# A segment-recurrent attention block with its gradients on one core: W_k held in two tiles, scaled O stored from GpSimd's queue, and the last forward step reordered

## Chip, core and metric

The kernel runs on one core of a Trainium2 chip. The metric is device time in microseconds (us) of one execution; lower is better. The engines are TensorE (PE in the profile; its weight loads are PEld), VectorE (DVE), ScalarE (ACT), GpSimd (POOL) and SyncE (SP), which issues most of the transfers. Transfers that GpSimd issues go through a queue of their own (q0, software), those of SyncE through another (q1, hardware).

## The reference

The program computes a transformer block and all its gradients. `x` is 2048 rows of 512; the attention part works in 64 segments of 32 rows, and 8 rows of memory go from one segment to the next, so the segments are a chain:

```python
mod = (_silu(c) @ w_mod).reshape(c.shape[0], 6, 1, -1)      # sa, ca, ga, sb, cb, gb
h = _layernorm(x, axis=-1) * (1 + ca) + sa
x = x + ga * _A_ref(h, A_mem0, A_Wq, A_Wk, A_Wv, A_Wo, A_seg_len)
h = _layernorm(x, axis=-1) * (1 + cb) + sb
x = x + gb * _B_ref(h, B_w_gate, B_w_up, B_w_down)
...
for s in range(n_seg):                                      # inside _A_ref, H = 32 heads of 128
    h = jnp.concatenate([mem, xs], axis=1)                  # 8 + 32 rows
    q = jnp.einsum('btd,dhe->bhte', h, Wq)
    k = jnp.einsum('btd,dhe->bhte', h, Wk)
    v = jnp.einsum('btd,dhe->bhte', h, Wv)
    p = _softmax(scores, axis=-1)                           # scores masked
    o = jnp.einsum('bhqk,bhke->bhqe', p, v)
    o = jnp.einsum('bhte,hed->btd', o, Wo)
    mem = o[:, :M, :].copy()
    outs.append(o[:, M:, :])
...
h = _sigmoid(g) * u                                         # _B_ref: g = x w_gate, u = x w_up
return jnp.einsum('bsf,fd->bsd', h, w_down)
```

The outputs are the block's result and the gradients of `x`, the memory, all weights and the modulation, for a given gradient of the result.

## The kernel before

One program in stages, on one core.

**Setup** (to about 50 us) loads the weights (W_q, W_k and W_v are 4 MB each) and starts the modulation vectors. `W_q` and `W_k` come in through a helper that loads heads 24 to 31 into a side tile first and later places them with VectorE copies (`place`).

**Forward loop** (`for s in range(NS)`, 64 steps of about 14 us, to about 950): q, k and v of one segment (`pass_ps` products with Wk, Wq and Wv in PE), scores `st_ps`, their exponentials `ET` (L902), the row sums and P V products `or_ps` (L906, L926), the scaled O `Ost` (VectorE L957 and ScalarE L954, by the reciprocal `rden`, L911), its transposes `tps` (L918), and the output product `at_ps` with Wo. `Ost` has one buffer. For the backward pass each step also stores scaled O as rows (`OSR`, L1089), O transposed (`OT`, L1127), V transposed (`VT`, L1154) and P (`PS`, L1155): 352 KB each, all in SyncE's queue, in which the two DMA transposes of the step stand too (VTr, L1051, and Pst, L1059). P is transposed by a DMA and scaled on GpSimd one step later (`norm`, L1152). The memory rows come back through `at_ft` and `hT`. In every fourth step a row tile of 128 rows goes through its first norm, and GpSimd stores it (`H1ROWS`, L419). Sixteen loads of modulation weights (`wmod_r`, L195) are spread over the loop.

**The last step, s = 63**, is written out apart: in it the weights of the second part are loaded over those of the first (`w_gate`, L996, and `w_up`, L1061, over Wk; `w_down`, L1086, over Wv), the first row tile of the second part is prepared (`first_tile`: its norm's power on GpSimd L776, its scaling on VectorE L779, a cast on GpSimd L780), step 62's P is scaled (L1152), and step 63's own P is transposed by PE (`turn_p`) and scaled by VectorE (`scale_p`, L946), then stored (L1160). The rows of the next tiles are loaded by `glu_load` (L1188 to L1191) in SyncE's queue.

**Second part** (950 to 1284): 16 row tiles forward and backward through w_gate, w_up and w_down; `hh` is transposed by a DMA (`hhT`, L1357, SyncE's queue) for the product with w_down (L1379). Then its weight gradients (L1583, to 1456), beside which the transposed weights of the backward loop are made by PE transposes (`wtp`, L1677).

**Backward loop** (1456 to about 2430): the segments in reverse. The first step's loads `Pst_l`, `VT_l`, `OT_l` (L1830), `Qst` and `Kst` (L1845) go into space that the second part has used; the pools p4ld (loads), p4pt and p4rx lie one behind the other, p4ld first, over Wv's space. `g_ps` (L1923) needs Pst_l and `dOst`, which GpSimd copies (L1968). A step's dq, dk and dv go out as rows (`DQR`, `DKR`, `DVR`, 352 KB each) in GpSimd's queue. At the end of a step the gradient of the memory rows is summed: the product `dhq_ps` with its last piece (`foldsel`), split in two halves `dh_hi` (ScalarE) and `dh_lo` (VectorE), folded by PE (`dh_ft`), copied to `dyT` (ScalarE, L2049), on which the next step's products wait. `proj_b` is a product of 16 matmuls (`pass_ps<-WoT,dyb`), which in most steps fills PE where it would wait.

**Last stage** (to 2974): the weight gradients of the attention.

The order of each engine's instructions is that in which the program issues them; `pin` keeps a scheduler from moving them. A transfer waits in its engine's order, so all that stands behind a waiting transfer of SyncE waits too.

Of the kernel before, what the change touches and what calls it, by code (L numbers as in the profile page):

```python
# [7 lines left out]
BF16 = mybir.dt.bfloat16  # L8
# [32 lines left out]
class K:  # L41
# [145 lines left out]
    def mod_rest(self, psp, pool, k):  # L187
# [5 lines left out]
        def load():  # L193
            st["w"] = pool.tile([128, DC, 128], BF16, name="wmod_r", bufs=1)
            nc.sync.dma_start(st["w"][:], self.io["w_mod"].rearrange("(cc p) n -> p cc n", p=128)[:, :, sl])  # L195
# [51 lines left out]
    def col_pass(self, psp, w, hf, lhs, rows, eng, ps=None, cs=None, steps=None):  # L247
# [5 lines left out]
        for c in cs or range(DC):  # L253
            wc = w[:, c, :].rearrange("p (h e) -> p h e", e=E)
# [14 lines left out]
    def load_heads(self, t, w, src, parts=1):  # L269
# [4 lines left out]
        n = 24 // parts  # L274
        for i in range(parts):
            nc.sync.dma_start(w[:, :, i * n * E:(i + 1) * n * E], src[:, :, i * n:(i + 1) * n, :].rearrange("p c h e -> p c (h e)"))

        def place():
            i = 24
            for hl in range(3):  # L280
                m = 3 if hl < 2 else 2
                nc.vector.tensor_copy(w[:, :, i * E:(i + m) * E].rearrange("p c (h e) -> p c h e", e=E),
                                      t[:, :, hl:hl + 3 * (m - 1) + 1:3, :])
                i += m
# [164 lines left out]
    def phase2(self):  # L449
# [9 lines left out]
        Wk = self.Wk = wvk.tile([128, DC, H * E], BF16, name="Wk")  # L459
# [5 lines left out]
        with ExitStack() as ctx:  # L465
# [391 lines left out]
            for s in range(NS):  # L857
# [178 lines left out]
                if s == NS - 1:  # L1036
                    v_chunk(s, 2)
                    first_tile[5]()
                st_exp(0)
# [20 lines left out]
                else:  # L1060
                    nc.gpsimd.dma_start(self.w_up, io["B_w_up"].rearrange("(c p) f -> p c f", p=128))  # L1061
# [23 lines left out]
                if s == NS - 1:  # L1085
                    nc.gpsimd.dma_start(self.w_down, io["B_w_down"].rearrange("(fc p) d -> p fc d", p=128))  # L1086
                    for g0, t, w in ((0, RAs[0]["k"], 8), (8, RAs[0]["q"], G - 8)):
                        nc.sync.dma_start(self.VT[s, :, g0:g0 + w, :], t[:, 0:w * GW].rearrange("p (g x) -> p g x", x=GW))
                nc.sync.dma_start(self.OSR[s], gl3(Ost))  # L1089
                at_ps = outproj()  # L1090
                if s == NS - 1:
                    nc.sync.dma_start(self.OT[s], gl3(OT))
# [4 lines left out]
                    parts = self.split_pair(sb2, at_ps, "at")  # L1097
                    while tail.pieces:
# [7 lines left out]
                    self.pop_later()  # L1106
                    self.pop_later()
                    turn_p(1)
                    self.pop_later()
                    for pi in (2, 0, 1):  # L1110
                        scale_p(pi)
# [35 lines left out]
                self.store_rows(psp, sb2, ft, self.AOA[s + 1, 0:32, :], "at", "p")  # L1147
                if s4 == nseg_t - 1:
# [11 lines left out]
            nc.sync.dma_start(self.PS[NS - 1], Pst[:])  # L1160
# [3 lines left out]
    def glu_tiles(self):  # L1164
# [6 lines left out]
        in_k = [self.flat(Wk, 2 * n + i * D, D) for i in range(4)]  # L1171
# [3 lines left out]
        self.w_gate = self.flat(Wk, 0, n).rearrange("p (c f) -> p c f", c=DC)  # L1175
        self.w_up = self.flat(Wk, n, n).rearrange("p (c f) -> p c f", c=DC)
# [17 lines left out]
    def phase3(self):  # L1194
# [9 lines left out]
        with ExitStack() as ctx:  # L1204
# [256 lines left out]
            dbr = self.flat(self.Wk, 0, NT * D).rearrange("p (j d) -> p j d", j=NT)  # L1461
            hr_0 = self.flat(self.Wk, NT * D, NT * 384).rearrange("p (j f) -> p j f", j=NT)
# [69 lines left out]
            accs = self.flat(self.Wk, 2 * DC * F, 2 * D, F32)  # L1532
# [7 lines left out]
        with ExitStack() as ctx:  # L1540
# [12 lines left out]
            h2r = self.flat(self.Wk, NT * D, NT * D).rearrange("p (j d) -> p j d", j=NT)  # L1553
# [97 lines left out]
    def p4_weights_setup_pieces(self, ctx):  # L1651
# [7 lines left out]
        slots = [self.flat(self.Wv, 2 * NT * 448, n)] + [self.flat(self.Wk, i * n, n) for i in range(3)]  # L1659
        first = [slots[0], self.flat(self.Wk, NT * D, n), slots[0], slots[0]]  # L1660
# [45 lines left out]
    def phase4(self):  # L1706
# [7 lines left out]
        with self.p4_ctx as ctx:  # L1714
            WqT, WkT, WvT, WoT, negones = self.WqT, self.WkT, self.WvT, self.WoT, self.negones

            ldp = ctx.enter_context(tc.tile_pool(name="p4ld", bufs=2, reuse_waits="tile"))
            pt = ctx.enter_context(tc.tile_pool(name="p4pt", bufs=1, reuse_waits="tile"))
            rxp = ctx.enter_context(tc.tile_pool(name="p4rx", bufs=3, reuse_waits="tile"))
# [79 lines left out]
            def proj_b(t, hf, parts=1):  # L1799
                ps = psb.tile([128, 512], F32, name="pass_ps", tag="dh")  # L1800
# [24 lines left out]
            def get_loads(s):  # L1825
                if s not in loads:
                    d = {}
                    for nm, dram in (("Pst", self.PS), ("VT", self.VT), ("OT", self.OT)):
                        t = ldp.tile([128, G * GW], BF16, name=nm + "_l")
                        (nc.scalar if s == NS - 1 and nm == "VT" else nc.sync).dma_start(gl3(t), dram[s])  # L1830
# [19 lines left out]
            nc.gpsimd.dma_start(self.DHA[NS, 0:M, :], dSs[0][0:M, 0:D])  # L1850
# [13 lines left out]
            for s in reversed(range(NS)):  # L1864
# [91 lines left out]
                def dht_pairs(X, WT):  # L1956
# [84 lines left out]
                pair = self.split_pair(sb2, dht_pairs(dQT, WqT), "dh")  # L2041
# [8 lines left out]
                g = s // 4  # L2050
# [470 lines left out]
```

## Time and profile before

| | us |
|---|---|
| median of 3 runs (lowest, highest) | 2974.27 (2969.84, 2976.05) |
| the profiled execution | 2976.26 |
| its span | 2974.5 |
| mean granted clock of PE, as a share | 0.998 |

The profile is of one execution. Its page gives each engine's busy time and, in the chain that ended last, what the end hangs on; the views behind it list who waited for whom, and the instructions in order of time (start, duration, engine, line, operation, and in brackets the idle time ahead with the instruction that ended it). A transfer's row in a queue (SPq, ACTq) is its issue; its data land later. Engine names in the rows are those above; `L` is a line of the kernel before.

### The profile page before, as it was taken

Reading aid. Unit: us, or ns where it says so; the run is one execution under the profiler, and the core shown is the slowest. Engines: PE = TensorE matmul, PEld = TensorE weight load, DVE = VectorE, ACT = ScalarE, POOL = GpSimd, SP = SyncE. Lnnn points to the kernel's source line nnn. Section 1 sums busy time; section 2 is a strip of 40 time slices with the busy share of each in tenths; the row PEclk is TensorE's granted clock in tenths of the full one; section 3 lists DMA queues with packets and bytes.
Section 4 is the critical chain, followed back from the end, with each engine's and each line's share of the span. In section 5 each row is a group of like instructions: output and inputs, shape, how many; then the busy total and the mean of one; then the engine's idle time right before and its main releaser. Section 6 shows DMA issues by size and latency. Waiting matters only on the chain.

```text
span 2974.5 us, 105438 instructions
## 1 busy us (share of the span) xinstructions
PE 2913.0 (98%) x43838; PEld 1818.8 (61%) x43838; DVE 1625.0 (55%) x3689; ACT 1340.7 (45%) x3234; POOL 1231.7 (41%) x2487
## 2 busy tenths in 40 slices
PE   6999999999998999999999999999999999999999
PEld 3666666666665444445677776777777754445545
DVE  5565565665555788733456665666566632850011
ACT  3666666666665444312355555555555520110011
POOL 2555555545545222221344444444444432762111
PEclk9999999999999999999999999999999999999999
DMA  9889988998899899998699999999999997786565
GB/s 308 221 226 220 219 220 223 219 216 220 211 228 275 210 231 229 239 284 276 193 248 259 246 255 238 253 250 253 252 253 253 250 278 245 250 265 191 161 215 172
DMA packets 838066, 703.01 MB, mean 236 GB/s; under 512 B 537698, under 2 KB 710162, under 8 KB 836692
## 3 DMA queue, kind: packets, MB, share of 16 engines
q1 hardware_dynamic: 711972, 485.29, 66.3%
q0 software_dynamic: 54512, 148.63, 15.9%
q10 hardware_dynamic: 71104, 62.34, 6.5%
q8 instruction: 345, 5.65, 0.8%
q14 instruction: 133, 1.09, 0.1%
HBM read 294.99 MB, written 276.35 MB: 192 GB/s over the span
## 4 chain that ended last, share of the span: by engine, by line
PE 88%; DMA 4%; issue 3%; DVE 2%; ACT 1%; POOL 1%; SPq 0%; DVEq 0%; POOLq 0%; ACTq 0%
PE gps L2300 14%; PE pass_ps L257 14%; PE dh_ps L215 8%; PE g_ps L1923 5%; PE pass_ps L677 5%; PE gps5o L2315 4%; PE dhq_ps L223 4%; PE at_ps L223 4%; PE dh_tps L215 3%; PE gps L1583 3%; PE mm L1404 2%; PE turn_ps L890 2%; PE tps L1840 2%; PE st_ps L900 1%; PE mm L1364 1%
## 5 line engine op out<-in xcount | busy, mean ns | idle before, releaser
L2300 PE MATMUL gps<-rows,hrows 128*128 128x512 bf16 (+2 forms) x2160 | 415.5, 355 | 0.0
L2300 PEld LDWEIGHTS <-hrows 128*128 128x128 bf16 x2160 | 211.1, 98 | 204.5 <-issue 0.9
L1152 POOL TENSOR_TENSOR Pst<-Pst,rden 120x1408 bf16<-120x1408 bf16 x63 | 159.7, 2535 | 344.5 <-issue 209.0
L63 DVE CAST ot<-gps 128x512 bf16<-128x512 f32 (+3 forms) x76 | 48.1, 633 | 308.2 <-PE gps L2300 222.5
L1968 POOL COPY dOst<-RAd 96x512 bf16<-96x512 bf16 x128 | 75.1, 611 | 298.9 <-DVE RAd L63 298.7
L61 ACT ACTIVATE ot<-gps 128x512 bf16<-128x512 f32 (+3 forms) x75 | 41.2, 549 | 348.2 <-PE gps L2300 220.1
L677 PE MATMUL pass_ps<-Wv,hT 128*32 128x512 bf16 (+2 forms) x2304 | 186.8, 357 | 0.0
L2304 POOL DMA_DIRECT2D out_dram<-ot x104 | 78.6, 756 | 255.8 <-DVE ot L63 129.5
L257 PEld LDWEIGHTS <-hT 128*32 128x32 bf16 x4096 | 117.2, 97 | 95.9 <-issue 5.7
L63 DVE CAST Vst<-pass_ps 96x512 bf16<-96x512 f32 x128 | 87.3, 682 | 106.2 <-ACT RBv L61 102.7
L215 PE MATMUL dh_ps<-WvT,dVT 128*32 128x512 bf16 x2048 | 134.5, 383 | 1.7 <-DVE RBd L63 0.2
L223 PE MATMUL at_ps<-Wo,OT 128*32 128x256 bf16 x4096 | 128.1, 276 | 1.3 <-DMA Wo<-in_A_Wo_dram 0.9
L677 PE MATMUL pass_ps<-Wv,hb 128*32 128x512 bf16 (+2 forms) x636 | 126.5, 339 | 0.2
L257 PE MATMUL pass_ps<-Wk,hT 128*32 128x512 bf16 x2048 | 122.7, 380 | 2.1 <-POOL hT L563 1.1
L257 PE MATMUL pass_ps<-WoT,dyT 128*32 128x256 bf16 (+1 forms) x3072 | 122.8, 308 | 1.0 <-ACT dyT L2049 0.9
L257 PE MATMUL pass_ps<-Wq,hT 128*32 128x512 bf16 x2048 | 123.2, 379 | 0.3 <-DVE RBk L63 0.3
L223 PE MATMUL dhq_ps<-WqT,dQT 128*32 128x256 bf16 x4096 | 123.1, 273 | 0.2 <-issue 0.2
L215 PE MATMUL dh_ps<-WkT,dKT 128*32 128x512 bf16 x2048 | 122.3, 380 | 0.0
L2315 PE MATMUL gps5o<-WoT,rows 128*128 128x512 bf16 x560 | 121.0, 379 | 0.0
L223 PEld LDWEIGHTS <-dQT 128*32 128x32 bf16 x4096 | 109.9, 97 | 16.1 <-issue 0.4
L317 DVE TENSOR_TENSOR dST<-dh_ps,dST 128x512 bf16<-128x512 f32 x64 | 44.3, 692 | 130.3 <-ACT dST L316 130.3
L1910 DVE SCALAR_TENSOR_TENSOR dS<-dp_ps,Pst_l 128x480 bf16<-128x480 f32 (+1 forms) x192 | 106.2, 608 | 12.4 <-PE dp_ps L1908 6.7
(480 smaller groups left out, 7040.3 us busy)
## 6 DMA issues: line engine op xcount, KB each, us to landing
OSR<-Ost SPq DMA_DIRECT2D x64, 352.0 KB
OT<-OT SPq DMA_DIRECT2D x64, 352.0 KB
PS<-Pst SPq DMA_DIRECT2D x64, 352.0 KB
Pst_l<-PS SPq DMA_DIRECT2D x64, 352.0 KB
OT_l<-OT SPq DMA_DIRECT2D x64, 352.0 KB
DVR<-rows_x POOLq DMA_DIRECT2D x64, 352.0 KB, 6.0
DKR<-rows_x POOLq DMA_DIRECT2D x64, 352.0 KB, 5.7
DQR<-rows_x POOLq DMA_DIRECT2D x64, 352.0 KB, 3.5
```

What stands on the lines that cost most here:

```text
L63: return nc.vector.tensor_copy(out, in_)
L215: self.nc.tensor.matmul(ps[32 * j:32 * j + 32, :], lhsT=lhsT, rhs=w, start=(n < 4), stop=(n >= total - 4), tile_position=(0, 32 * j))
L223: nc.tensor.matmul(ps[32 * j:32 * j + 32, :], lhsT=x[k], rhs=w[k][:, 256 * d:256 * d + 256], start=(n == 0), stop=(n == total - 1), tile_p ...
L257: self.nc.tensor.matmul(ps[32 * j:32 * j + 32, :], lhsT=lhs(c), rhs=rhs, start=(c == 0), stop=(c == DC - 1), tile_position=(0, 32 * j))
L677: nc.tensor.matmul(ps[32 * j:32 * j + 32, o * E:(o + n) * E], lhsT=lhsT, rhs=wc[:, 3 * a + hl:3 * (a + n - 1) + hl + 1:3, :], start=(c == ...
L1152: nc.gpsimd.tensor_tensor(Pst[0:120, :, :], Pst[0:120, :, :], rden[:, :].unsqueeze(2).to_broadcast([120, G, 128]), op=ALU.mult)
L1583: nc.tensor.matmul(ps[:], lhsT=h2r[:, j, c * 128:(c + 1) * 128], rhs=xr[:, j, :], start=(j == 0), stop=(j == NT - 1))
L1910: nc.vector.scalar_tensor_tensor(out=part3(dS, pi)[:, :, 0:120], in0=ps[:, 0:n, 0:120], scalar=cfg.scale, in1=part3(Pst, pi)[:, :, 0:120], ...
L1923: nc.tensor.matmul(ps[:, j, 0:w], lhsT=lh[:, g * GW:(g + 1) * GW], rhs=rh[:, g * GW:g * GW + w], start=True, stop=True)
L2300: nc.tensor.matmul(ps[:, 0:ng * E], lhsT=hrows[:, tp_, c * 128:(c + 1) * 128], rhs=rows[:, tp_, 0:ng * E], start=(tp_ == 0), stop=(tp_ == ...
L2304: (nc.sync if i == len(todo) - 1 else nc.gpsimd).dma_start(outw[c * 128:(c + 1) * 128, h0:h0 + 3 * (ng - 1) + 1:3, :], ot[:, 0:ng * E].rea ...
L2315: nc.tensor.matmul(pss[gg][:], lhsT=rows[:, t, gg * E:(gg + 1) * E], rhs=dyrows[:, t, :], start=(n == 0), stop=(n == NTP - 1))
```

## The change

- W_k becomes two tiles of half the rows each (`Wk0`, `Wk1`); the loading helper, the products with W_k and the placing copies work on either. What lay in W_k's space (w_gate, w_up, the rings, buffers of the weight gradients) lies in one or the other.
- The backward loop's pools are opened in another order, so that the first loads lie in Wk0's space; VT_l's first load goes to SyncE's queue, and the first DHA store from GpSimd's queue to SyncE's.
- OSR's store moves from SyncE's queue to GpSimd's in steps 0 to 62, behind the store of the memory rows and the copy of O's tail, ahead of the next copies and of `norm`; the loads of modulation weights move to GpSimd's queue.
- Last step: w_up is issued behind w_gate, w_down behind the first tile's cast, step 62's `norm` behind both (so the power comes ahead of it); the last OSR store stays in SyncE's queue; P is scaled by ScalarE, group by group, into the step's V buffer.
- In steps 63 and 62 of the backward loop, 8 of proj_b's matmuls go ahead of the last piece of `dhq_ps` and 8 behind it, ahead of `dh_ft`; they stood behind `dh_ft`.

```diff
-            nc.sync.dma_start(st["w"][:], self.io["w_mod"]...)
+            nc.gpsimd.dma_start(st["w"][:], self.io["w_mod"]...)
...
-        Wk = self.Wk = wvk.tile([128, DC, H * E], BF16, name="Wk")
+        Wk = self.Wk = [wvk.tile([128, DC // 2, H * E], BF16, name=f"Wk{i}") for i in range(2)]
...
                 def scale_p(pi):
-                    n = min(PG, G - pi * PG)
-                    nc.vector.tensor_tensor(Pst[0:120, pi * PG:pi * PG + n, :], turned_p[pi][0:120, 0:n, :],
-                                            rden[:, pi * PG:pi * PG + n].unsqueeze(2).to_broadcast([120, n, 128]), op=ALU.mult)
+                    for j in range(min(PG, G - pi * PG)):
+                        g = pi * PG + j
+                        nc.scalar.activation(Vst[0:120, g * GW:(g + 1) * GW], turned_p[pi][0:120, j, :], AF.Copy,
+                                             scale=rden[:, g:g + 1])
...
                     nc.gpsimd.dma_start(self.w_gate, io["B_w_gate"].rearrange("(c p) f -> p c f", p=128))
-                    norms.pop()()
+                    nc.gpsimd.dma_start(self.w_up, io["B_w_up"].rearrange("(c p) f -> p c f", p=128))
...
                     first_tile[5]()
+                    nc.gpsimd.dma_start(self.w_down, io["B_w_down"].rearrange("(fc p) d -> p fc d", p=128))
+                    norms.pop()()
...
-                else:
-                    nc.gpsimd.dma_start(self.w_up, io["B_w_up"].rearrange("(c p) f -> p c f", p=128))
...
-                    nc.gpsimd.dma_start(self.w_down, io["B_w_down"].rearrange("(fc p) d -> p fc d", p=128))
...
-                nc.sync.dma_start(self.OSR[s], gl3(Ost))
                 at_ps = outproj()
                 if s == NS - 1:
+                    nc.sync.dma_start(self.OSR[s], gl3(Ost))
...
                     parts = self.split_pair(sb2, at_ps, "at")
+                    scale_p(2)
...
                 self.store_rows(psp, sb2, ft, self.AOA[s + 1, 0:32, :], "at", "p")
+                nc.gpsimd.dma_start(self.OSR[s], gl3(Ost))
...
-            nc.sync.dma_start(self.PS[NS - 1], Pst[:])
+            nc.sync.dma_start(self.PS[NS - 1], gl3(Vsts[(NS - 1) % 2]))
...
+            rxp = ctx.enter_context(tc.tile_pool(name="p4rx", bufs=3, reuse_waits="tile"))
+            pt = ctx.enter_context(tc.tile_pool(name="p4pt", bufs=1, reuse_waits="tile"))
             ldp = ctx.enter_context(tc.tile_pool(name="p4ld", bufs=2, reuse_waits="tile"))
-            pt = ctx.enter_context(tc.tile_pool(name="p4pt", bufs=1, reuse_waits="tile"))
-            rxp = ctx.enter_context(tc.tile_pool(name="p4rx", bufs=3, reuse_waits="tile"))
...
-                        (nc.scalar if s == NS - 1 and nm == "VT" else nc.sync).dma_start(gl3(t), dram[s])
+                        nc.sync.dma_start(gl3(t), dram[s])
...
-            nc.gpsimd.dma_start(self.DHA[NS, 0:M, :], dSs[0][0:M, 0:D])
+            nc.sync.dma_start(self.DHA[NS, 0:M, :], dSs[0][0:M, 0:D])
...
+                    between()
                     self.pair_mm(ps, [self.foldsel[:, :]] * 2, parts, H // 2, H // 2 + 1)
...
+                def begin_b():
+                    if s >= NS - 2:
+                        begun.append(proj_b(g - 1, 3 - s4, 2, psp, "p"))
+
+                pair = self.split_pair(sb2, dht_pairs(dQT, WqT, begin_b), "dh")
+                begun = [f() for f in begun]
...
                 if s >= NS - 2:
-                    proj_b(g - 1, 3 - s4)()()
+                    begun.pop()()
```

More of the change, by code (lines that the diff above doesn't have):

```diff
@@ L1174, in glu_tiles @@
         self.ring_dout = [in_v[6], in_k[2], in_k[3], *in_v[7:10]]
-        self.w_gate = self.flat(Wk, 0, n).rearrange("p (c f) -> p c f", c=DC)
-        self.w_up = self.flat(Wk, n, n).rearrange("p (c f) -> p c f", c=DC)
+        self.w_gate, self.w_up = (self.flat(w, 0, n).rearrange("p (c f) -> p c f", c=DC) for w in Wk)
         self.w_gateT = self.flat(Wq, 0, n).rearrange("p (c d) -> p c d", c=FC)
@@ L1658, in p4_weights_setup_pieces @@
         n, NT = DC * HB * E, cfg.NT
-        slots = [self.flat(self.Wv, 2 * NT * 448, n)] + [self.flat(self.Wk, i * n, n) for i in range(3)]
-        first = [slots[0], self.flat(self.Wk, NT * D, n), slots[0], slots[0]]
+        slots = [self.flat(self.Wv, 2 * NT * 448, n)] + [self.flat(self.Wk[0], i * n, n) for i in range(3)]
+        first = [slots[0], self.flat(self.Wk[1], 0, n), slots[0], slots[0]]
         np_ = [0]
@@ L1797, in turn, with proj_b @@
                     to_heads(eng, tp[:], i0, 2, 0, 32, 0)
-            def proj_b(t, hf, parts=1):
-                ps = psb.tile([128, 512], F32, name="pass_ps", tag="dh")
+            def proj_b(t, hf, parts=1, pool=psb, tag="dh"):
+                ps = pool.tile([128, 512], F32, name="pass_ps", tag=tag)
                 def part(k):
```

39 lines of the change are left out of this document (22 added, 17 removed).

## The prediction

> **What bounds the kernel now.** First the page: the engines' busy time and the chain that ended last.
>
> ```profile
> span 2974.5 us, 105438 instructions
> ...
> PE 2913.0 (98%) x43838; PEld 1818.8 (61%) x43838; DVE 1625.0 (55%) x3689; ACT 1340.7 (45%) x3234; POOL 1231.7 (41%) x2487
> ...
> PE 88%; DMA 4%; issue 3%; DVE 2%; ACT 1%; POOL 1%; SPq 0%; DVEq 0%; POOLq 0%; ACTq 0%
> ```
>
> TensorE (PE) is busy for 2913.0 of 2974.5 us. The change adds no matmul and drops none; so it can only win or lose inside the 61.5 us in which PE stands. Next view: who made PE wait, over the whole span (us in total, times, longest).
>
> ```profile
> PE tps L918 <- DVE Ost L957: 8.9, 24, 1.1
> ...
> PE mm L1379 <- DMA hhT<-hh: 3.1, 1, 3.1
> ...
> PE dh_ft L242 <- ACT dh_hi L230: 2.0, 4, 0.5
> ...
> PE tp L1242 <- DMA Wv<-in_B_w_down_dram: 1.1, 1, 1.1
> ...
> PE mod_ps L200 <- DMA wmod_r<-in_w_mod_dram: 0.8, 2, 0.4
> ```
>
> The edits aim at these five rows and at two more that come below: the forward loop's scaled O (8.9) and modulation weights (0.8), w_down and hhT in the first tiles behind the loop (1.1 and 3.1), and the first backward steps (2.0). I ask of each how much really goes.
>
> **The change part by part.** *Scaled O's store to GpSimd's queue (63 of 64, all but the last step's) and 16 loads of modulation weights.* Ost is one buffer, so the next step may write it only when the store OSR<-Ost has landed. A row of the tile OSR's view (who waited for it: ScalarE, 6.2 us in 7 times), PE's waits from 50 to 930, and then the timeline of one step:
>
> ```profile
>   ACT Ost L954: 6.2, 7
> ```
> ```profile
> PE tps L918 <- DVE Ost L957: 7.6, 22, 1.1
> ```
> ```profile
> 564.32 0.27 POOL L563 COPY hT<-hx 128x96 bf16<-128x96 bf16 x1
> ...
> 566.54 0.90 SPq L1089 DMA_DIRECT2D OSR<-Ost  x1
> ...
> 569.57 2.53 POOL L1152 TENSOR_TENSOR Pst<-Pst,rden 120x1408 bf16<-120x1408 bf16 x1 [4.98 <-issue]
> ...
> 571.86 0.69 DVE L957 TENSOR_TENSOR Ost<-or_ps,rden 120x512 bf16<-120x512 f32 x1
> ...
> 572.61 0.39 PE L918 MATMUL tps<-ident,Ost 120*128 120x120 bf16 x4 [0.16 <-DVE Ost L957]
> ```
>
> SyncE comes to the store at 566.54, behind its two DMA transposes, 5.3 us ahead of the next write at 571.86. On GpSimd it stands just ahead of the hT copy: 564.32, so 2.2 us sooner and 7.5 us ahead of the write. What it costs there: 63 issues, which delay the hT copy and all behind it by one issue each; GpSimd stands 4.98 us ahead of the next product (569.57), which covers that nine times over. The price and the landing of a 352 KB store on that queue I take from the backward's, of the same size and shape (issue ns and landing us, least, median, most):
>
> ```profile
> L2025 POOL DMA_DIRECT2D DVR<-rows_x x64: 539/569/572, 1468.5 to 2404.9; - x64
> ...
> DMA to landing us min/median/max: 4.7/6.0/8.3
> ```
>
> 0.57 us of issue, landed after 6.0 of the 7.5 us at hand: the wait goes. How much is that on PE? The 7.6 us are 22 waits; row 572.61 shows one of 0.16 us where nobody waited for a store, the plain length of DVE's chain. Taking 22 times 0.16 = 3.5 off leaves 4.1. The modulation's 0.8 may go or stay; I take half. Term: **-4.5**; ends -8.4 (all of 7.6 and 0.8) and 0, and below that the rival of slower.
>
> The row that would speak against it is GpSimd's issue beside a busy VectorE (the step's small stores from 540 to 600, ns of one: least, median, most):
>
> ```profile
> L847 POOL DMA_DIRECT2D Vst<-RBv x12: 502/530/585, 543.3 to 585.1; - x12
> ```
>
> VectorE is busy for 55% of the span (first fence), and no issue of these twelve took over 585 ns. The Trainium skill, page "SBUF — State Buffer", section "SBUF: two separate sides", says that a GpSimd DMA's descriptors cannot be written while VectorE holds their shared port: 620 ns become some 3100. By that rule, an estimate from this page, the landing would be 2.5 us later; the issue times here do not show it.
>
> *The last forward step (s = 63).* Five edits meet: the power of the first tile's norm goes ahead of step 62's P product on GpSimd, w_up and w_down are loaded sooner, step 62's OSR goes ahead of w_gate, and step 63's P is scaled by 11 ScalarE instructions instead of 3 of VectorE. Timeline of PE, VectorE, GpSimd and SyncE's queue, then the chain of waits:
>
> ```profile
> 935.71 1.69 PE L677 MATMUL pass_ps<-Wv,hT 128*32 128x512 bf16 x24
> ...
> 941.23 0.21 PE L906 MATMUL or_ps<-ones,ET 128*128 128x1 bf16 x3 [1.55 <-DVE rden L911]
> ...
> 942.91 0.38 PE L918 MATMUL tps<-ident,Ost 120*128 120x120 bf16 x4 [0.95 <-DVE Ost L957]
> ```
> ```profile
> 939.85 0.55 DVE L779 TENSOR_SCALAR RBv<-x,st 128x512 f32<-128x512 f32 x1 [2.36 <-POOL st L776]
> ```
> ```profile
> 936.74 2.53 POOL L1152 TENSOR_TENSOR Pst<-Pst,rden 120x1408 bf16<-120x1408 bf16 x1 [3.90 <-issue]
> ...
> 945.09 1.10 POOL L1086 DMA_DIRECT2D Wv<-in_B_w_down_dram  x1
> ```
> ```profile
> 942.15 1.14 ACT L954 ACTIVATE Ost<-or_ps,rden 120x128 bf16<-120x128 f32 x4 [2.89 <-DMA OSR<-Ost]
> ```
> ```profile
> 960.78 0.33 SPq L609 DMA_DIRECT2D KST<-RA1k  x1
> ...
> 969.60 3.05 SPq L1357 DMA_TRANSPOSE hhT<-hh  x1
> ```
> ```profile
> 933.34 9.67 DMA OT<-OT
> ```
>
> The 1.55 us: VectorE stood 2.36 us for the power, which stood behind the 2.53 us product. With the power first it goes. The 0.95: Ost waited for step 62's store, as ScalarE's 2.89 shows; ahead of w_gate on GpSimd it goes too. So PE comes out of the step 2.5 us sooner, and with w_down's issue some 6 us earlier (behind Wv's last reader, 935.71 + 1.69 = 937.4, instead of 945.09) the 1.1 us at w_down go as well: 3.6. The P product, now behind w_down, ends near 937.4 + 1.1 + 2.5 = 941.0; its store waits for step 62's OT anyway, which lands at 933.34 + 9.67 = 943.0, so that move costs nothing. ScalarE's 11 scalings cost 11 times 1.14 / 4 = 3.1 us, in a stretch where it is free (view below: 4.53 and 5.32 of 10 us busy).
>
> What is late next? The transposes hhT, which PE then waits for. They stand in SyncE's queue behind a string of stores and loads that begins when step 63's OT has landed (960.78) and goes on without a pause for 8.8 us. And OT lands when the DMA engines have moved what is ahead of it:
>
> ```profile
> 940.00:950.00 10.00, 7.62 (x136) 5.13 (x135) 4.93 (x13) 4.53 (x11) 6.84 (x11) 0.83 0.97 337
> 950.00:960.00 10.00, 8.24 (x64) 4.48 (x60) 7.52 (x16) 5.32 (x10) 4.84 (x9) 1.00 1.01 390
> ```
>
> The last columns are PE's granted clock, the DMA share and GB/s: the engines are full (0.97 and 1.01), and the edits reorder the bytes without sparing any. So hhT goes out at nearly the same time, and most of the 3.6 us come back as a longer wait at L1379. Term: **-1** (OT's store is issued some 2 us sooner, and half of that may survive); ends -5 (the 3.6, and 0.17 of 7.6 busy us, 1.3, if the clock stays up) and +2 (weights in front of the stores).
>
> *First backward loads.* The pools are laid out anew, so that Pst_l, VT_l and the first OT_l lie in the first tile of W_k:
>
> ```profile
> 1449.34 0.39 PE L1677 MATMUL wtp<-ident,Wk 128*128 128x128 bf16 x4
> ...
> 1455.90 0.34 SPq L1830 DMA_DIRECT2D Pst_l<-PS  x1
> ...
> 1458.21 0.53 POOL L1850 DMA_DIRECT2D DHA<-dS  x1
> 1458.73 1.17 POOL L1968 COPY dOst<-RAd 96x512 bf16<-96x512 bf16 x2
> ...
> 1460.29 0.37 PE L1923 MATMUL g_ps<-Pst_l,dOst 128*128 128x120 bf16 x4 [1.62 <-DMA Pst_l<-PS]
> ```
>
> They then wait only for the last transposes that read it, 1449.7 instead of 1455.90. What is late next: the dOst copies, which the same product needs. Without the DHA store (0.53, now SyncE's) they end at 1459.4 instead of 1459.9. PE starts there, 0.9 us sooner. Term **-0.9**, ends -1.6 (the whole wait) and 0.
>
> *proj_b in steps 63 and 62 of the backward.*
>
> ```profile
> 1470.75 0.28 PE L223 MATMUL dhq_ps<-dST,foldsel 128*32 128x256 bf16 x4
> ...
> 1472.18 1.05 PE L257 MATMUL pass_ps<-WoT,dyb 128*32 128x512 bf16 x16
> 1472.29 0.20 ACT L2049 ACTIVATE dyT<-dh_ft 128x32 bf16<-128x32 f32 x1 [0.82 <-PE dh_ft L242]
> ...
> 1473.06 1.91 PE L257 MATMUL pass_ps<-WoT,dyT 128*32 128x512 bf16 x48
> ```
>
> Its 16 matmuls (0.88 us from start to start, 0.055 each) covered PE's wait for dyT; now 8 stand ahead of the foldsel product and 8 behind it. The chain foldsel, dh_hi, dh_lo, dh_ft, dyT takes 1472.49 - 1470.75 = 1.74 us, its handing over included about 1.8. It starts 8 times 0.055 = 0.44 us later, so the dyT products begin 2.24 us after the old start of foldsel instead of 2.31. Of the two steps' stalls (half of the 2.0 above) almost nothing is won: **-0.1**, ends -1.4 and +0.2.
>
> *The start.* W_k's load in twice as many pieces, and other semaphores for W_v and W_q behind it:
>
> ```profile
> 0.00:50.00 50.00, 30.02 (x335) 14.48 (x335) 30.31 (x80) 13.01 (x27) 13.42 (x48) 1.00 1.00 363
> ```
>
> The DMA engines are full (1.00) for 50 us; the same bytes take the same time. Term **0**, ends -1 and +2, a pause in the queue. Setup, both weight-gradient stages and the rest of the backward keep PE's order: 0.
>
> Sum: -4.5 - 1 - 0.9 - 0.1 = **-6.5**. The profiled execution took 2976.26 us (span 2974.5), 2.0 over the median 2974.27 of the runs. 2976.3 - 6.5 = 2969.8 by the one, 2967.8 by the other; I say **2969**.
>
> **The rivals.** *All of it comes.* OT lands 4 us sooner and hhT with it, every Ost wait goes: -8.4 - 5 - 1.6 = -15, or 2961. For it: w_gate and w_up no longer leave a gap. Against it: the DMA share is already 0.97 to 1.01.
>
> *The store's wait comes back.* If the landing on GpSimd's queue takes as much longer as the issue is sooner (6.0 becomes 7.5 and more in many steps), forward gives 0 and there remains -2: 2974. For it: both queues share the same engines. Against it: the store no longer stands behind SyncE's transposes.
>
> *Slower: GpSimd's landing.* Every fourth step, such as the one quoted, GpSimd comes late to the store, behind the norm of the next row tile (16 tiles); there the budget is 7.5 us. Each us of landing beyond it is a us of PE. At 8.3, the longest above, that is 16 times 0.8 = 13 us, and 13 - 2 = 11 us slower, 2987; it decides against the kernel by over 6 us from a mean landing of 8.0 in these steps (16 times 0.5 = 8, less 2). By the Trainium skill's rule above (SBUF — State Buffer) it would come to just that. Against: the median of 6.0 comes from the backward's steps, where GpSimd's queue carries three such stores a step (dV, dK and dQ).
>
> **How the numbers follow.** Forecast (-3 to -10): 0.5. All of it: 0.15. The wait comes back: 0.25. Slower: 0.1. The range leaves out the far half of the first and most of the last: 2961 to 2978. A measurement of this kernel tells about 0.2%, 6 us, from no change, so below 2968.3 counts as faster: 0.15 and somewhat over half of the forecast's 0.5, 0.43. Slower than 2980.2: 0.11. Between: 0.46.
>
> **What would show it.** Right: no engine waits for OSR<-Ost from 50 to 930 and PE's wait at L918 is near 3.5 us; its landing there is about 6 us; or_ps and w_down are gone from PE's waits, and the one for hhT has grown by 2 to 3 us; g_ps starts 0.9 us sooner, bound by dOst; in the first two backward steps PE waits for dyT in place of dh_hi. Wrong: OSR<-Ost still named by VectorE or ScalarE, with landings over 7.5 us; hhT issued 4 us sooner; a PE wait at the start that was not there.

## The result and the profile after

| | kernel before | changed kernel |
|---|---|---|
| median of 6 runs, us (lowest, highest) | 2972.85 (2969.84, 2977.20) | 3032.45 (2992.12, 3050.16) |
| ratio, 95% interval | | 1.0164 [1.0132, 1.0196] |
| the profiled execution / its span, us | 2976.26 / 2974.5 | 3036.81 / 3035.0 |

The change makes the kernel slower, by 1.3 to 2.0%. (The ratio leaves out two slow executions of the changed kernel's six, and so is not the quotient of the medians.) The changed kernel also spreads over 58 us where the other spreads over 7.

The page of the changed kernel: span, engines, the chain that ended last, and the store that was moved, with its time to landing as the last figure.

```profile
span 3035.0 us, 105299 instructions
...
PE 2932.1 (97%) x43838; PEld 1819.9 (60%) x43838; DVE 1628.8 (54%) x3689; ACT 1343.7 (44%) x3245; POOL 1285.2 (42%) x2565
...
PE 62%; issue 3%; DMA 2%; ACT 1%; DVE 1%; POOL 1%; SPq 0%; DVEq 0%; POOLq 0%; ACTq 0%
...
OSR<-Ost POOLq DMA_DIRECT2D x63, 352.0 KB, 5.5
```

PE has the same 43838 matmuls and now stands for 3035.0 - 2932.1 = 102.9 us instead of 61.5. That is 41 of the 60.5 us by which the span grew; in the other 19 PE is busy, with the same work. The store lands in 5.5 us, sooner than the 6.0 that I counted on; and yet this is where the loss comes from. Who made PE wait, whole span:

```profile
PE at_ft L242 <- ACT at_hi L230: 30.8, 17, 3.4
PE tps L923 <- DVE Ost L963: 16.4, 26, 2.6
...
PE ao_tps L215 <- POOL ao_tail L2393: 2.9, 1, 2.9
...
PE gps5o L2129 <- DMA rows<-OSR: 2.5, 1, 2.5
...
PE mm L1385 <- DMA hhT<-hh: 1.9, 1, 1.9
```

The first row was 1.5 us before, and the wait for Ost, which was to go, has nearly doubled (8.9 before). Both lie in the forward loop. From ScalarE's hT copy of step 0 to that of step 62 the traces show 55.39 to 929.94 before and 55.16 to 987.30 after: 874.6 and 932.1 us, 58 us more. From there to the end it is 2044.6 and 2047.7.

In this stretch PE has 17261 matmuls in both kernels. It stands for 52.5 instead of 12.6 us, 40 us more: 29 of them wait for at_hi (1.5 before, 30.8 after), 7 for Ost (7.6 and 14.6), 4 for at_lo. And it is busy for 879.6 instead of 861.9 us, 18 us more, at a lower granted clock. 200 us of the loop, before and after (the first pair is PE's busy time and matmuls, the third figure from the end the clock):

```profile
250.00:450.00 200.00, 198.76 (x4017) 131.92 (x4018) 121.54 (x299) 135.11 (x357) 104.71 (x211) 1.00 0.89 218
```
```profile
250.00:450.00 200.00, 191.40 (x3776) 124.61 (x3769) 114.47 (x277) 127.24 (x333) 113.11 (x228) 0.98 0.88 209
```

That is 49.5 and 50.7 ns of busy time a matmul. The clock goes with PE's standing in this loop: 12.6 us and 1.00 in the kernel before, 28.6 and 0.99 in osr_sp_front below, 52.5 and 0.98 here, 77.8 and 0.97 in before_ps_mid. So each us of standing went with some 0.4 us of slower work; what sets the clock no run separates.

One bad step shows the way, from SyncE over GpSimd and ScalarE to PE. First the kernel before, in the step that answers to it (SyncE's queue, then GpSimd):

```profile
572.13 0.32 SPq L1155 DMA_DIRECT2D PS<-Pst  x1
...
577.60 2.02 SPq L1059 DMA_TRANSPOSE Pst<-ET  x1
579.72 0.53 SPq L1089 DMA_DIRECT2D OSR<-Ost  x1
```
```profile
581.55 2.53 POOL L1152 TENSOR_TENSOR Pst<-Pst,rden 120x1408 bf16<-120x1408 bf16 x1 [5.36 <-issue]
```

Then the changed kernel (SyncE, GpSimd, ScalarE, PE):

```profile
603.72 0.32 SPq L1162 DMA_DIRECT2D PS<-Pst  x1
...
610.12 2.83 SPq L1067 DMA_TRANSPOSE Pst<-ET  x1
```
```profile
607.53 0.56 POOL L1154 DMA_DIRECT2D OSR<-Ost  x1
...
615.88 2.54 POOL L1159 TENSOR_TENSOR Pst<-Pst,rden 120x1408 bf16<-120x1408 bf16 x1 [7.52 <-DMA Pst<-ET]
618.37 1.56 POOL L852 DMA_DIRECT2D Vst<-RBv  x3
619.92 0.65 POOL L65 COPY kT<-b_colsk 128x192 bf16<-128x192 bf16 x3
```
```profile
620.60 0.60 ACT L61 ACTIVATE b_colsk<-turn_ps 128x512 bf16<-128x512 bf16 x1 [2.93 <-POOL kT L65]
621.10 0.38 ACT L230 ACTIVATE at_hi<-at_ps 128x256 bf16<-128x256 f32 x1
```
```profile
621.53 0.27 PE L242 MATMUL at_ft<-foldsel,at_hi 128*128 128x32 bf16 x4 [2.03 <-ACT at_hi L230]
```

Read upwards: PE waits for at_hi, which stands on ScalarE behind a copy that waits for GpSimd's kT copies (once in four steps such a buffer is refilled); these stand on GpSimd behind the scaling of P, and the scaling waited 7.52 us for P's DMA transpose, issued at 610.12. From issue to scaling it is 5.8 us here and 3.95 in the step before the change. OSR was issued 2.6 us ahead of that transpose, at 607.53, and takes 5.5 us to land (median), so for some 3 us the two run side by side ahead of the landing; before, OSR was issued 2.1 us behind the transpose, in the same queue.

There is a **round** in this: GpSimd scales P of a step; SyncE, which has waited for that, stores it (PS) and goes on to the K and Q stores and the next two transposes; P's transpose lands; GpSimd scales the next P. One tile Pst makes it a chain. The mean of its four pieces over steps 8 to 59 (starts and ends of the rows above, taken step by step) gives the table that the experiments are read by:

| us | issue of P's transpose to scaling | scaling | to PS | PS to next transpose | round | step (hT to hT) |
|---|---|---|---|---|---|---|
| before | 5.02 | 2.53 | 0.67 | 5.84 | 14.06 | 14.08 |
| changed | 6.39 | 2.54 | 0.24 | 5.88 | 15.05 | 15.03 |

Each of these rows comes once a step, so the four pieces add up to a step in every kernel; that the sum equals the step does not show that the round bounds anything. What tells is whether somebody in it has time to spare. GpSimd stood idle ahead of the scaling in all 52 steps of both kernels. From PS to the next transpose SyncE issues without a break (0.7 us of gaps, over six issues, in both). Ahead of PS SyncE had stood for over 0.3 us, waiting for the scaling, in 26 of the 52 steps before and in 37 after. So this chain was closed in half of the steps before, and in most of them after. Its first piece became 1.37 us longer, 0.43 of that came back ahead of PS, and the step is 0.95 us longer: 52 times 0.95 makes 49 us of the loss.

### The profile page after: what moved, and what is told of

It reads as the page before. It is cut to its first block, busy times and chain, and to the rows that moved or that the text cites. A ratio compares the mean times of both kernels' runs of the same rounds, so it can differ in the third digit from the quotient of the medians.

```text
span 3035.0 us, 105299 instructions
## 1 busy us (share of the span) xinstructions
PE 2932.1 (97%) x43838; PEld 1819.9 (60%) x43838; DVE 1628.8 (54%) x3689; ACT 1343.7 (44%) x3245; POOL 1285.2 (42%) x2565
## 4 chain that ended last, share of the span: by engine, by line
PE 62%; issue 3%; DMA 2%; ACT 1%; DVE 1%; POOL 1%; SPq 0%; DVEq 0%; POOLq 0%; ACTq 0%
PE gps L2314 14%; PE dh_ps L215 8%; PE g_ps L1929 5%; PE pass_ps L257 5%; PE gps5o L2329 4%; PE dhq_ps L223 4%; PE mm L1410 3%; PE dh_tps L215 3%; PE mm L1385 2%; PE mm L1370 2%; PE tps L1846 1%; PE mm L1339 1%; PE gps L1589 1%; PE mm L1343 1%; PE gps L1488 1%
## 5 line engine op out<-in xcount | busy, mean ns | idle before, releaser
L257 PE MATMUL pass_ps<-Wk,hT 128*32 128x512 bf16 x2048 | 134.7, 409 | 2.1 <-DVE mv L409 1.1
```

Of the source, the lines that this page charges most:

```text
L257: self.nc.tensor.matmul(ps[32 * j:32 * j + 32, :], lhsT=lhs(c), rhs=rhs, start=(c == 0), stop=(c == DC - 1), tile_position=(0, 32 * j))
```

## The experiments

**Theory A:** OSR in GpSimd's queue runs beside P's transpose, lengthens the round, and the round bounds the loop. **Rivals:** B, the time that 79 more issues take on GpSimd; C, W_k's halves and other addresses; D, it is only a second queue that costs; E, the queue slows everything, whatever the order of SyncE; F, GpSimd's queue alone takes the larger part of the DMA engines. The round itself is lengthened and shortened through SyncE's order; a second buffer for Pst, which would open it, was not tried. Each ratio is to the kernel before, run beside it on the same chip (its medians there: 2969.1 to 2972.1). Round and step agree in every row, as they must; the two pieces, from issue to scaling and from PS to the next transpose, are what to read.

| run | us (lowest, highest) | ratio to before, 95% | issue to scaling | PS to next | round | step |
|---|---|---|---|---|---|---|
| undo_osr | 2976.86 (2972.58, 2984.91) | 1.0024 [1.0014, 1.0034] | 5.22 | 5.95 | 14.13 | 14.15 |
| osr_alone | 3029.13 (3027.05, 3039.17) | 1.0205 [1.0186, 1.0223] | 6.04 | 6.12 | 15.01 | 14.97 |
| wmod_alone | 2975.74 (2971.24, 2979.00) | 1.0015 [1.0005, 1.0025] | 5.28 | 5.88 | 14.17 | 14.21 |
| osr_sp_front | 3004.77 (3002.67, 3006.22) | 1.0117 [1.0100, 1.0133] | 4.72 | 6.71 | 14.44 | 14.47 |
| osr_act | 3051.95 (3039.72, 3059.41) | 1.0265 [1.0233, 1.0297] | 6.51 | 6.11 | 15.34 | 15.45 |
| osr_half | 3003.28 (3000.42, 3009.75) | 1.0108 [1.0086, 1.0130] | 5.40 | 5.98 | 14.57 | 14.59 |
| after_ps_mid | 3039.91 (3035.64, 3052.20) | 1.0235 [1.0209, 1.0261] | 4.05 | 4.41 | 15.05 | 14.96 |
| before_ps_mid | 3062.98 (3057.70, 3067.30) | 1.0305 [1.0284, 1.0326] | 3.98 | 4.12 | 15.66 | 15.58 |
| after_kq_last | 2981.93 (2972.24, 2986.48) | 1.0040 [1.0028, 1.0051] | 6.12 | 4.53 | 14.28 | 14.22 |
| before_kq_last | 2978.09 (2974.23, 2983.20) | 1.0028 [1.0017, 1.0038] | 4.95 | 4.90 | 14.25 | 14.18 |
| rest_only | 2973.40 (2969.65, 2978.67) | 1.0009 [1.0000, 1.0018] | 4.95 | 5.79 | 14.00 | 14.05 |

### Which part it is

undo_osr, on the changed kernel:

```diff
-                nc.gpsimd.dma_start(self.OSR[s], gl3(Ost))
...
+                nc.sync.dma_start(self.OSR[s], gl3(Ost))
                 at_ps = outproj()
```

> The change with one part undone: OSR's 63 stores back in SyncE's queue at their old place; all else as changed. Theory A (round): P's round of a step (DMA transpose of ET, GpSimd's scaling, SyncE's store, next transposes) takes nearly a step, and OSR in GpSimd's queue runs beside the transposes and lengthens it. A expects 2964 to 2974 us, P's transpose to its scaling again about 5 us from issue (5.5 to 7 in the change), no wait of PE for at_hi worth 29 us. Rival B (GpSimd's time: 79 more issues and the weight loads ahead of its copies) expects a good part to stay, over 2985, since the 16 weight loads stay. Rival C (the halves of W_k, other addresses) expects nothing to come back: 3010 to 3050.

osr_alone is the same edit the other way round, on the kernel before:

> The kernel before with this one part: OSR's stores of steps 0 to 62 in GpSimd's queue at the changed place, weight loads and all else as before. Theory A expects the whole loss: 3010 to 3055 us. Rival B expects a part of it, since 63 of 79 issues are there but no weight load stands among them: 2985 to 3020. Rival C expects 2968 to 2975.

wmod_alone, on the kernel before:

```diff
-            nc.sync.dma_start(st["w"][:], self.io["w_mod"]...)
+            nc.gpsimd.dma_start(st["w"][:], self.io["w_mod"]...)
```

> The kernel before with this one part: the 16 loads of modulation weights in GpSimd's queue. Theory A expects 2968 to 2976 us (four of 64 KB... in all 2 MB over 64 steps, nothing beside the transposes most of the time). Rival B expects 2985 or more, a third of the loss.

The store alone makes the whole loss, and without it the loss is gone but for 4 to 10 us (undo_osr came out 3 us over the range of theory A). PE's and ScalarE's waits of osr_alone, 50 to 930:

```profile
PE at_ft L242 <- ACT at_hi L230: 25.5, 14, 3.1
```
```profile
ACT b_colsk L61 <- POOL kT L65: 38.5, 15, 4.0
```

C falls. B falls as to its size, and what stays is theory A in small: the 16 weight loads (128 KB each) are issued beside the transposes of the third of every four steps, and there the way from P's transpose to its scaling grows most, from 5.05 to 5.74 us in wmod_alone and to 5.72 in undo_osr (in the first of the four by 0.2 to 0.3 us, in the others by under 0.1). PE's wait for Ost grew with it, in wmod_alone (7.6 us before):

```profile
PE tps L918 <- DVE Ost L957: 13.3, 28, 1.2
```

### Is it GpSimd's queue, or bytes ahead of or beside the transpose?

osr_sp_front, on the kernel before:

```diff
-                    nc.sync.dma_start(VTr[:], Vst[:, :], transpose=True)
...
-                    nc.sync.dma_start(Pst[:], ET[:, :], transpose=True)
...
                 nc.sync.dma_start(self.OSR[s], gl3(Ost))
+                if s < NS - 1:
+                    nc.sync.dma_start(VTr[:], Vst[:, :], transpose=True)
+                    nc.sync.dma_start(Pst[:], ET[:, :], transpose=True)
```

> The kernel before with SyncE's order changed alone: OSR's store goes ahead of the step's two DMA transposes instead of behind them; all stays in SyncE's queue. Theory A says that what counts is when P's transpose lands: with 352 KB ahead of it in its own queue it lands 1 to 2 us later, the round grows past the step, and the time is 2995 to 3050 us, with PE waiting for at_hi in every fourth step. Rival D (only a second queue beside the transposes costs, a queue's order does not) expects 2968 to 2978.

osr_act, on the kernel before, in steps 0 to 62:

```diff
-                nc.sync.dma_start(self.OSR[s], gl3(Ost))
...
+                nc.scalar.dma_start(self.OSR[s], gl3(Ost))
```

> The kernel before with OSR's stores of steps 0 to 62 in ScalarE's hardware queue, at the place in the step at which the change has them on GpSimd. Theory A (bytes beside the transposes, whichever queue) expects a loss of the same kind, P's transpose 5.5 to 7 us from issue to scaling, 2995 to 3050. Rival F (GpSimd's queue with its own descriptors takes the larger part of the engines) expects 2965 to 2980.

osr_half, on the kernel before, in steps 0 to 62:

```diff
-                nc.sync.dma_start(self.OSR[s], gl3(Ost))
+                nc.sync.dma_start(self.OSR[s, :, 6:, :], gl3(Ost)[:, 6:, :])
...
+                nc.gpsimd.dma_start(self.OSR[s, :, 0:6, :], gl3(Ost)[:, 0:6, :])
```

> The kernel before with 6 of 11 groups of OSR (192 of 352 KB) in GpSimd's queue at the changed place and the rest in SyncE's at the old one. Theory A: issue to scaling between 5.0 and 6.2, about 5.6 us; the round then exceeds the step by less: 2985 to 3010. A price for each store on GpSimd whatever its size would give 3020 to 3035.

D falls: 352 KB ahead of the transposes in SyncE's own queue cost 34 us. But P's transpose didn't become slower there, as I had expected (4.72 us to its scaling, 5.02 before); the round is longer by its other piece (5.84 to 6.71, SyncE's issues). F falls: ScalarE's hardware queue does no less harm than GpSimd's. Some of its loss is its own: the issue stands in ScalarE's order, and between 50 and 930 PE waits 3.8 us for ScalarE's copies behind it (turn_ps and st_ps), which it did not before. Half the bytes cost about half. PE's waits for at_hi, in this order of the runs (50 to 930):

```profile
PE at_ft L242 <- ACT at_hi L230: 14.2, 11, 2.6
```
```profile
PE at_ft L242 <- ACT at_hi L230: 28.3, 13, 3.9
```
```profile
PE at_ft L242 <- ACT at_hi L230: 12.4, 12, 1.5
```

### Is it the round?

after_ps_mid and before_ps_mid, each on the kernel of its name:

```diff
                     nc.sync.dma_start(VTr[:], Vst[:, :], transpose=True)
+                    if ps_late:
+                        ps_late.pop()()
...
-                    nc.sync.dma_start(self.PS[s], Pst[:])
+                    ps_late.append(lambda: nc.sync.dma_start(self.PS[s], Pst[:]))
```

> The changed kernel with the round shortened: SyncE issues the store of P (PS) of the step before behind the K and Q stores and V's transpose, just ahead of P's next transpose, instead of ahead of them all; so SyncE no longer holds these five up while GpSimd scales. OSR stays in GpSimd's queue, beside the transposes. Theory A (the round of P is what bounds the changed loop) expects most of the loss back: P's transpose still 6 to 6.5 us from issue to scaling, but the round under 14 us, and 2970 to 2995. Rival E (the stores in GpSimd's queue slow all transfers, whatever the order) expects 3015 to 3050, no change.

> The same reordering of SyncE in the kernel before. Theory A: before, the round just fits into the 14 us step and costs little; SyncE comes sooner to OSR, so the waits for Ost (7.6 us) may go: 2963 to 2972. Rival E: 2968 to 2975, nothing.

Both expectations missed (after_ps_mid fell into rival E's range, but with P's transpose at 4.05 us, not at the 6 and more that I had expected of it), and the reason was one that I had left out: P's transpose writes the tile that PS still reads. SyncE's own waits, of before_ps_mid:

```profile
SPq L1062 <- DMA PS<-Pst: 178.3, 55, 4.9
```

PS has to have landed, about 4.1 us after its issue; issued later, it holds the transpose up, and the step of the kernel before becomes 15.6 us with OSR in its old place. This is a loss without any move to another queue, but PE meets it elsewhere. Its waits of before_ps_mid, 50 to 930:

```profile
PE tps L919 <- DVE Ost L958: 58.9, 42, 4.0
...
PE at_ft L242 <- ACT at_hi L230: 0.9, 4, 0.2
```

The OSR store stands behind the transpose in SyncE's queue, and Ost waits for it. So this run shows what SyncE's standing still costs; it does not show the way over GpSimd and at_hi.

after_kq_last and before_kq_last, on the same two kernels, leave PS in front and take the four K and Q stores out of the way:

```diff
-                        rows_out(RA[x], DR[x], s, 1)
+                        kq_late.append(lambda: rows_out(RA[x], DR[x], s, 1))
...
                     nc.sync.dma_start(Pst[:], ET[:, :], transpose=True)
+                    while kq_late:
+                        kq_late.pop(0)()
```

> The changed kernel with P's round shortened at another place: SyncE issues the four K and Q stores of a step behind its two transposes instead of ahead of them. The run before showed that P's transpose also waits until the store PS of the step before has landed (about 4 us from its issue), so the store stays first and only the four issues between (some 3 us) go. OSR stays on GpSimd. Theory A: PS to the next transposing of P shrinks from 5.9 to about 4.2 us, the round to 13 to 13.5 us against a step of 14, PE's wait for at_hi goes, 2968 to 2995. Rival E (OSR's queue slows all, whatever the order) expects 3015 to 3050.

> The same reordering in the kernel before: the round, 14.06 us long beside steps of 14.08, gets slack of 1 to 2 us. Theory A: SyncE is never late to OSR for this reason; Ost's waits (7.6 us) shrink unless the K and Q stores ahead of OSR take the place: 2964 to 2973. Rival E: no change, 2968 to 2975.

This decides between A and E. In after_kq_last OSR is still on GpSimd and P's transpose still slow (6.12 us), but PS to the next transpose is 4.53 instead of 5.88, and in it SyncE now stands for 2.3 us instead of 0.7: the round has time to spare. Of the 60 us between the medians 50 are back (by the ratios, 37 of 49), and the clock in the loop is 1.00 again. The round of 13 to 13.5 us that I had expected could not show: the sum is the step, 14.2 us. PE's wait for at_hi, 50 to 930:

```profile
PE at_ft L242 <- ACT at_hi L230: 5.4, 7, 2.6
```

In the kernel before the reordering doesn't pay: 9 us more (2978.09 against 2969.21 on the same chip), outside both expectations. There the four stores come between the transposes and OSR, as the expectation had feared, and PE's wait for Ost grows from 8.9 to 18.9 us (whole span):

```profile
PE tps L919 <- DVE Ost L958: 18.9, 28, 3.5
```

### What the rest of the change does

rest_only, on the changed kernel, undoes both moves to GpSimd's queue (the two diffs above, backwards). rest_old_pools takes rest_only and opens the pools p4ld, p4pt, p4rx in the old order.

> The change without its two moves to GpSimd's queue: OSR and the modulation's weights on SyncE, all else as changed (W_k in two tiles, the last step, the first backward loads, proj_b). The sum on record without its forward term: -1 for the last step, -0.9 for the first loads, -0.1 for proj_b: 2967 to 2973. If the last step's gain were not taken back by hhT: 2964 to 2967. If W_k's halves or the start cost something: over 2974.

> The run before it (the change without its two moves to GpSimd's queue) with the backward loop's pools opened in the old order, so that the first loads lie over Wv again and the buffers of the row stores stand last. In all five runs with the new order the stretch from the last dyT to the end took 583.8 to 585.7 us, in the six with the old one 579.6 to 580.2, and PE waited 2.5 to 4.5 us for rows<-OSR, whose load waited for the last row stores (DKR, DQR) to land. Theory G: the new order makes that load wait for these stores' buffers. G expects 579.5 to 580.5 us in that stretch, no wait of PE for rows<-OSR, some 0.8 us lost again at the first g_ps, and a time of 2964 to 2970, 2 to 5 us under the kernel before by the last step's gain. The rival (the wait belongs to W_k's halves or to some other part) expects 583 us or more there and 2970 to 2975.

last_only puts the last step's edits alone on the kernel before (w_up, w_down, `norm` and ScalarE's scaling as in the diff of the change); last_osr62 has step 62's OSR on GpSimd besides:

> The kernel before with the last forward step's edits alone: the norm's power ahead of step 62's scaling, w_up behind w_gate, w_down behind the first tile's cast, P scaled by ScalarE. No W_k halves, no move of OSR or of the modulation's weights, old pools. From the last hT of the loop to the first product with hhT: 43.7 to 43.9 us in the runs with these edits and OSR on SyncE, 44.8 to 47.8 in those without. Theory H (the last step itself gives 1 to 4 us, and what the remainder lost was W_k's halves and the pools): 43.5 to 44.5 us there, 579.6 to 580.2 from the last dyT on, and 2965 to 2970. The rival (the 4 us are a draw of the run, as the spread of 44.8 to 47.8 may say) gives 2969 to 2973.

> The same with step 62's OSR alone on GpSimd, ahead of w_gate. There is no next round of P that its bytes could lengthen: no transposes of step 63 follow. Theory A with H expects the wait of the last Ost for its store to go and 0 to 1 us less than the run beside it, 2964 to 2970. If GpSimd's queue cost by itself, 1 us or more is lost.

| run | us (lowest, highest) | ratio to before, 95% | hT of step 62 to first hhT product | last dyT to the end |
|---|---|---|---|---|
| before (its profiled execution) | | | 47.81 | 580.2 |
| rest_only | 2973.40 (2969.65, 2978.67) | 1.0009 [1.0000, 1.0018] | 43.85 | 585.7 |
| rest_old_pools | 2973.39 (2967.13, 2978.67) | 1.0003 [0.9993, 1.0013] | 43.94 | 582.0 |
| last_only | 2971.32 (2965.86, 2982.88) | 1.0010 [0.9998, 1.0021] | 40.64 | 579.9 |
| last_osr62 | 2974.11 (2966.25, 2979.34) | 1.0016 [1.0005, 1.0027] | 40.76 | 579.7 |

Without the moves the change is worth nothing that can be measured. The expected times of these four runs were all missed, by 0.4 to 4 us. The traces show a last step that is shorter and an end that is longer. How much shorter is open: the 47.81 us of the kernel before are one execution, and two kernels without the last step's edits have 44.84 (wmod_alone) and 44.89 (before_kq_last). PE's waits of rest_only over its end, and SyncE's (2380 to 2430):

```profile
PE gps5o L2128 <- DMA rows<-OSR: 4.5, 1, 4.5
```
```profile
SPq L2110 <- DMA DKR<-rows_x: 5.8, 1, 5.8
```

With the new order of the pools SyncE's load of the last stage's first rows waits for the last row stores, and PE for the load: 2.5 to 4.5 us in every kernel with that order, at most 0.5 in those with the old one and an undivided W_k. That was on no list of mine. That the order makes it is only half shown. With the old order 2.2 of the 4.5 us are still there, SyncE still waits 4.1 us for DKR, and in the kernel before its load waits for a row store too (DQR, 6.3 us), without PE waiting. The first backward step lost 4 us from its first g_ps to dyT (12.2 to 16.4), and the median didn't move. PE's waits of rest_old_pools over its end:

```profile
PE gps5o L2328 <- DMA rows<-OSR: 2.2, 2, 2.0
```

last_only's profiled execution is the shortest of all (span 2963.8), yet its median is no lower than that of before (2969.08 beside it); last_osr62 differs from it by less than the intervals. Whether the last step's gain is there in the mean stays open. Neither version beats the kernel before.

## Why the prediction was wrong

*Scaled O's store, -4.5 us:* this step failed, with its sign. Two sentences of it carried the mistake. "GpSimd stands 4.98 us ahead of the next product (569.57), which covers that nine times over": the idle time was no slack. GpSimd waited there for P's transpose, in a chain that had no time to spare in half of the steps. And "landed after 6.0 of the 7.5 us at hand: the wait goes": the landing was right (5.5 us measured), but I asked only whether the store itself is in time, not what its 352 KB run beside. They run beside P's transpose, 5.02 us becomes 6.39, and the loop is 58 us longer: 40 us of PE standing and 18 of PE working at a lower clock, which the prediction had for the last step alone ("if the clock stays up").

*The rival of slower* had the smaller part: landing beyond the time at hand. That did happen, in nine steps. Who waited for OSR in the changed kernel, and its landing:

```profile
  DVE Ost L963: 11.8, 9
...
DMA to landing us min/median/max: 3.1/5.5/9.4
```

At PE it is the 7 of the 40 us that wait for Ost; the 29 at at_hi are the mechanism it missed. The prediction's own sign of being wrong, OSR<-Ost still named with landings over 7.5 us, did appear. The Trainium skill's rule on the shared port (page "SBUF — State Buffer", section "SBUF: two separate sides") did not show here: the 63 issues took 542 to 607 ns. What bears on the result is its page "DMA: Bandwidth & Descriptors", section "Issuing engines are not separate DMA queues": transfers of all queues run on the same 16 engines and interleave, and another queue saves only issue time. osr_act agrees: from ScalarE's queue, the same bytes at the same place in the step cost 2.3 to 3.0%.

*The modulation's loads, half of 0.8 us:* wrong in sign too, 0.05 to 0.25% slower by themselves, for the same reason.

*The last step, -1 us:* the two waits (1.55 and 0.95) are gone in rest_only and last_only. The one for w_down (1.1 before) is gone in last_only alone, and is 1.4 in rest_only. PE still ends up waiting for hhT, but this wait, which was to grow by 2 to 3 us from 3.1, shrank to 2.7 and 1.5 us: the step "most of the 3.6 us come back" did not show. Whether -1 was the right size stays open: hhT goes out 36.9 us after the hT of step 62 in rest_only and 39.7 in the kernel before, but also after 37.0 and 37.3 in before_kq_last and wmod_alone, which lack these edits, and the medians show no gain. "That move costs nothing" failed in the changed kernel itself, where the scaling of step 62, late by its round, stood behind w_down and held up what follows (GpSimd, then PE):

```profile
1001.27 2.79 POOL L1159 TENSOR_TENSOR Pst<-Pst,rden 120x1408 bf16<-120x1408 bf16 x1 [3.78 <-issue]
```
```profile
1005.10 1.91 PE L215 MATMUL ao_tps<-Wo,ao_tail 128*32 128x512 bf16 x32 [2.90 <-POOL ao_tail L2393]
```

*First backward loads, -0.9 us:* right, with the limit named, and a little small. The loads go out 9 us ahead of the product, and g_ps waits for dOst; from the last transpose of wtp to g_ps it is 5.5 us instead of 6.9. SyncE and PE of the changed kernel:

```profile
1506.20 0.34 SPq L1836 DMA_DIRECT2D Pst_l<-PS  x1
```
```profile
1515.33 0.38 PE L1929 MATMUL g_ps<-Pst_l,dOst 128*128 128x120 bf16 x4 [0.22 <-POOL dOst L1975]
```

But PE waited 2.5 us here (4.5 in rest_only) for rows<-OSR at the other end of the backward loop, which I put down as 0 ("the rest of the backward").

*proj_b, -0.1 us:* right. PE now waits for dyT, and from foldsel to the dyT products it is 1.78 us (1.8 forecast):

```profile
1526.01 0.28 PE L223 MATMUL dhq_ps<-dST,foldsel 128*32 128x256 bf16 x4
...
1527.24 0.27 PE L242 MATMUL dh_ft<-foldsel,dh_lo 128*128 128x32 bf16 x4 [0.19 <-DVE dh_lo L232]
1527.79 1.92 PE L257 MATMUL pass_ps<-WoT,dyT 128*32 128x512 bf16 x48 [0.29 <-ACT dyT L2064]
```

## What to carry to other kernels

Before a transfer is moved to another queue, look for what lands in the same microseconds, and walk the round in which that stands. Look at each link for time to spare; that the pieces add up to a step says nothing, for they always do. Where each link begins as soon as the one before has ended, most of what is added to one piece is added to the step (here 0.95 of 1.37 us), however idle the engines on it look. An engine that is idle "for issue" ahead of an instruction has slack only if nothing that ends there has come late. And a changed order of pools has two ends: see what is freed first, but also what is then freed last.

## What the runs showed of the hardware

- A 352 KB store beside a DMA transpose of 352 KB lengthened the transpose's way from issue to use by 1.0 to 1.5 us, and its issue on SyncE from 2.02 us (kernel before) to 2.84 (osr_alone) and 3.02 (osr_act); from GpSimd's software queue and from ScalarE's hardware queue alike.
- A store of 352 KB on SyncE's queue held its source for about 4.1 us (before_ps_mid, from PS's issue to the transpose that waited for it).
- In the forward loop PE's granted clock fell as PE stood longer: 1.00 at 12.6 us of standing (kernel before), 0.99 at 28.6 (osr_sp_front), 0.98 at 52.5 (changed kernel), 0.97 at 77.8 (before_ps_mid); the same 17261 matmuls took 861.9 to 889.1 us of busy time.
- The six executions of the changed kernel lie 58 us apart; other kernels with a step over 14.5 us lay 9 to 20 us apart in four executions each. Why the changed one spreads so far was not found.
